# Moving the first batch's result stores to ScalarE's queue, and another order for the last projection

## The chip, the cores and the metric

The kernel runs on 1 core of one Trainium2 chip. The metric is the device time of one execution in microseconds (us). The engines are TensorE (PE for its matmuls, PEld for its weight loads), VectorE (DVE), ScalarE (ACT), GpSimd (POOL) and SyncE (SP, which here only issues DMAs). ACT and POOL can issue DMAs from their own queues too. Each engine works through its own list of instructions in order.

## The reference

Eight sequences of 3008 tokens and 256 channels pass through a spectral filter, and every token then passes through a gated feed-forward block:

```python
X = np.fft.rfft(x, axis=1)
Y = X * (filt_r + 1j * filt_i)[None]
y = np.fft.irfft(Y, n=3008, axis=1).reshape(8 * 3008, 256)
g = y @ w_gate                                   # 256 -> 1536
silu = g * (1.0 / (1.0 + np.exp(-g)))
out = (silu * (y @ w_val)) @ w_out               # 1536 -> 256
```

## The kernel before, in words

**Steps.** The feed-forward part of a batch is cut into 4 chunks of tokens (`k`) and the hidden width into 3 groups (`g`). One pair (k, g) is one step, so a batch has 12 steps and the kernel 96, and a last half step finishes what is left. In the first batch the first nine steps run over the chunks 0 to 2 for g = 0, then for g = 1, then for g = 2, and steps 9 to 11 are chunk 3; in the other batches the three groups of a chunk follow each other. In each step pieces of the next batch's Fourier work (`pa`, `pb`, `pc`, `pd`) are woven in. Steps are counted from 0 over the whole kernel.

**The order inside a step** is written out by hand: `SCHEDULE` (line 88) is a list of tokens, and each token emits a few instructions in this order to whichever engines do them. `P`, `Q`, `A`, `B`, `E` are products on PE (line 862); `f`, `c`, `m`, `g`, `u` are ACT's copies and activations out of PSUM; `D` (line 879) and `S` (line 913) are subtractions and additions on POOL; `s`, `x03`, `y`, `e`, `h`, `v`, `l` are mostly DVE. `W1` to `W7` are the seven products of the output projection (line 954) and `o1` to `o7` move or add a PSUM bank into the output tile (lines 966 and 968); `z0` to `z3` transpose its four parts in place on DVE (line 930), and `x0` to `x5` store the tile to DRAM, two DMAs each (line 943). A token with a prime belongs to the group two steps back (`older`) or to the previous group (`before`), as its place in the pipeline demands. So when a group's last hidden part is done in step s, its output is complete at the beginning of step s + 2 and is stored there, which happens for g = 2 alone.

**Queues of the stores.** Each of the 12 DMAs of a group stores up to 32 partitions in runs of 128 bytes. For the first batch they are issued from POOL, for the others from SP, and for the very last group they go around SP, ACT and POOL, in two halves (`x` and `X`). In the first batch groups with g = 2 are the steps 6, 7, 8 and 11, and their stores are issued in the steps 8, 9, 10 and 13, behind POOL's `S00'` and `S01'` and between its next subtractions.

**Preparation.** During the steps of the first batch the weights are rounded piece by piece. Line 1206 lets 20 ticks of that work happen in each step, at places spread evenly over the number of tokens in `SCHEDULE`.

**Banks of the projection.** `W1`, `W6`, `W7`, `W4` add up in one PSUM bank A, which `o1`, `o6`, `o7`, `o4` read in between; `W2` uses bank F, and `W5` and `W3` bank G. A product that adds into a bank waits until the reader before it is done. `S0` to `S3` make the four sums of the hidden tiles that `W5`, `W6`, `W7` and `W3` read. `LAST` (line 99) is the order of this for the final group; there all eight sums are on DVE (line 1246).

Of the kernel before, what the change touches and what calls it, by code (L numbers as in the profile page):

```python
# [64 lines left out]
NG = 3  # L65
# [20 lines left out]


SCHEDULE = """
Q0 o3' z1.o' t4.2' W2 f0 S00' S01' x0.o' t0.0 x1.o' Q1 t0.1 x2.o' P3 x3.o' f1 t4.3' W1 x4.o' S10' x03 S11'
s13 x5.o' P1 o1 t0.2 P0 o2 z0.o c1 D01 A13 g1 c0 S20' Q2 S21' g0 y01 m13 t1.0 h0 f2 s01 W6 t1.1 h1 x23  # L90
D02 P2 o6 D12 A01 c2 B13 g2 n3' m01 t0.3 S30' t1.2 x02 W7 S31' g13 y12 y02 B01 h13 o7 t1.3 t2.0 s02
s12 g01 h2 Q3 t2.1 h01 e12 A02 y23 W4 e02 y03 m02 g3 A12 o4 z2.o t2.2 E12 m12 B02 t2.3 l12 E02 u12 e13
g02 t3.0 h3 s23 l02 B12 v12 E13 t3.1 h02 u02 A23 n2 l13 g12 v02 W5 s03 e23 h12 e01 m23 A03 o5
z3.o u13 E23 t3.2 m03 v13 E01 l23 e03 t3.3 t4.0 l01 u23 B23 v23 u01 t4.1 E03 n1 v01 g23 B03 l03 W3 h23 g03
u03 h03 v03
""".split()
KS = (-1, 0, 1, 2)

LAST = """
S00 S01 S10 S11 W1 o1 W2 o2 z0.o S20 S21 S30 S31 W6 o6 W5 o5 W3 o3 z1.o x0.o x1.o x2.o x3.o x4.o  # L100
x5.o W7 o7 z3.o W4 o4 z2.o X0.o X1.o X2.o X3.o X4.o X5.o
""".split()
BLOCKS = (0, 1, 3, 2)
PAIRS = ((0, 1), (1, 2), (2, 3), (0, 2), (1, 3), (0, 3))
# [68 lines left out]
def kernel(  # L173
# [10 lines left out]
    nc = tc.nc  # L184
# [70 lines left out]
    def add(eng, dst, a, b):  # L255
        return eng.tensor_tensor(out=dst, in0=a, in1=b, op=ALU.add)  # L256
# [561 lines left out]
    def takes_turns(b, k):  # L818
        return b == 0 and k < NT

    def new_outs(b, k, g):
        outs[b, k] = opool.tile([128, 4 * NH, RP], FP32, name=f"o_{b}_{k}_{g}", tag="o", bufs=2)
        if g:
            pin(nc.sync.dma_start(out=outs[b, k], in_=o_dram[k]))
        else:
            pin(nc.gpsimd.memset(outs[b, k][:, :, NR:], 0.0))

    class Group:
# [94 lines left out]
        def project(self, op, last=False):  # L923

            b, k, q = self.b, self.k, self.g
            kind, p = op[0], int(op[1])
            if kind == "z":
                if q == NG - 1:
                    t = self.part(p)
                    pin(nc.vector.transpose(out=t, in_=t))  # L930
                return
            if kind in "xX":
                t, first, count = outs[b, k], 2 * NH * (kind == "X"), 2 * NH if last else 4 * NH
                if q < NG - 1 and takes_turns(b, k) and p == 5:
                    pin(nc.sync.dma_start(out=o_dram[k], in_=t))
                if q == NG - 1:
                    for n, (u, cq) in enumerate(divmod(m, 4) for m in (2 * p, 2 * p + 1)):
                        rows = min(32, NR - 32 * u)
                        at = (b * S + 32 * 32 * u + 2 * NH * k) * C + 128 * first + 32 * cq
                        queue = nc.sync if b else nc.gpsimd  # L940
                        if last:
                            queue = (nc.sync, nc.scalar, nc.gpsimd)[(2 * p + n) % 3]
                        pin(queue.dma_start(  # L943
                            out=bass.AP(tensor=out.tensor, offset=out.offset + at,
                                        ap=[[32 * C, rows], [128, count], [1, 32]]),
                            in_=t[32 * cq:32 * cq + rows, first:first + count, ts(u, 32)]))
                return
            at = {1: "A", 6: "A", 7: "A", 4: "A", 2: "F", 5: "G", 3: "G"}[p]
            if kind == "W":
                start = p in (1, 2, 5)  # L950
                if start:
                    self.bank(at, 3)
                for i in range(JB):
                    pin(nc.tensor.matmul(  # L954
                        out=self.tiles[at], lhsT=wo_t[:, JB * q + i, WO[p], :],
                        rhs=self.hs[i][:, HID[p]], start=start and i == 0,
                        stop=True, skip_group_check=True))
                return
            if q == 0 and p == 1:
                new_outs(b, k, q)  # L960
            i, cb = {1: (0, 0), 2: (0, 0), 6: (0, 1), 3: (0, 1), 4: (1, 0), 7: (1, 1),
                     5: (1, 1)}[p]
            dst = self.part(2 * i + cb)[:, :, 0:NR].rearrange("p n (t r) -> p t n r", t=2)
            src = self.tiles[at].rearrange("p (t n r) -> p t n r", t=2, n=NH)
            if q == 0 and at == "A":
                pin(nc.scalar.copy(out=dst, in_=src))
            else:
                pin(add(nc.vector, dst, dst, src))
# [7 lines left out]
    x0 = [t[0:NR, 8 * C * i:8 * C * i + 8 * C] for t, i in ((wo_f, 0), (wo_f, 1), (y_f, 0))]  # L976
    x0 = [t.rearrange("p (n c) -> p n c", c=C) for t in x0]
# [6 lines left out]
    with tc.tile_pool(name="start", bufs=1) as spool0:  # L984
# [3 lines left out]
        f0 = spool0.tile([128, NS, C], FP32, name="f0")  # L988
# [8 lines left out]
        n = 0  # L997
# [68 lines left out]
        for p in ("A13", "A01"):  # L1066
            at = SLOT[p]
# [29 lines left out]
    older = before = None  # L1097
    pieces_before = []

    def order_of(b):  # L1100

        steps = [divmod(step, NG) for step in range(NCHUNK * NG)]
        if b == 0:
            steps[:NT * NG] = [(k, g) for g in range(NG) for k in range(NT)]
        return steps
# [45 lines left out]
    for b in range(B):  # L1151
# [36 lines left out]
        for step in range(NCHUNK * NG + (b == B - 1)):  # L1188
            ghost = step == NCHUNK * NG
            k, g = order_of(b)[min(step, NCHUNK * NG - 1)]  # L1190
            this = None
            pieces = []
            if not ghost:
                pieces = plan[step]
                this = Group(b, k, g, cur.y[k], sequence_of(cur, nxt, step))
                if b == 0:
                    preparation.finish(step)
                chunk = {0: 1, 2: 2, 5: 3}.get(step)
                if b and chunk:
                    cur.load_t4(chunk, 0)  # L1200
            elif before is None:
                break
            ends = {ORDER[e - 1]: n for n, (_, e) in enumerate(PIECES)}
            last = ghost or b == B - 1 and step == NCHUNK * NG - 1
            for place, token in enumerate(SCHEDULE):
                if b == 0 and this and place * TICKS % len(SCHEDULE) < TICKS and \
                        (step or place > SCHEDULE.index("A01")):
                    preparation.tick(step)
                old = token.endswith("'")
                op = token.rstrip("'")  # L1210
                if op[0] == "t":
                    n = int(op[1])
                    ps = pieces_before if old else pieces
                    if n < len(ps):
                        next(ps[n], None)
                elif op[0] in "Wo" or op.endswith(".o"):

                    g0 = older if old else before
                    if g0 is not None and (old or not ghost):
                        g0.project(op)  # L1220
                else:
                    g0 = before if old else this
                    if g0 is not None and not (ghost and op[0] == "S"):
                        g0.step(op)
                if old or this is None:
                    continue
                if nxt and (step, op) == ((4, "P2") if b else (5, "A23")):
                    nxt.load_two(0)
                if b + 2 < B and (step, op) in ((10, "Q2"), (10, "B01"), (11, "Q2")):

                    following.load_x(2 if step == 11 else int(op == "B01"))
                if b + 2 < B and step == 11 and op in ("A02", "B02"):
                    following.pair(int(op == "B02"))
                if b and chunk and op == "B01":
                    cur.load_t4(chunk, 1)
                for i in range(2):
                    if nxt and (step, op) == (10, ("A12", "E23")[i] if b else "E23"):
                        nxt.load_t4(0, i)
                for f, args in chores.get((step, op), ()) if b == 0 else ():
                    f(*args)  # L1240
                if op in ends and not last and (b or step >= NT * NG - 1):
                    reload_weights((g + 1) % NG, ends[op])
            older, before, pieces_before = before, this, pieces
    for op in LAST:
        if op[0] == "S":
            older.step(op, nc.vector)
        else:
            older.project(op, True)
# [28 lines left out]
```

## Time and profile before

| | us |
|---|---|
| median of 7 runs (lowest to highest) | 2897.09 (2895.87 to 2899.42) |
| the profiled execution, its own time | 2896.33 |
| its span in the profile | 2894.6 |
| busy in the span: PE, DVE, ACT, POOL | 2843.9, 2075.3, 1577.8, 1532.0 |
| 48 stores of the first batch, POOL's time for one: least, median, most | 0.651, 0.664, 0.838 |
| 8 stores of the last group on ACT: least, median, most | 0.374, 0.466, 0.493 |

The profile lists for stretches of time how long each engine was busy, and in its timeline what each engine did in order, with the idle time before an instruction and what ended it in brackets. An instruction that only issues a DMA is shown as ACTq or SPq; POOL's DMA issues appear as POOL's own time. The share behind "DMA" is the mean busy share of the 16 DMA engines.

### The profile page before, as it was taken

The numbers are of one execution on the slowest core, as the hardware profiler recorded it, in microseconds if no ns is written. First come the engines' busy times: TensorE is split into PE (matmuls) and PEld (weight loads), VectorE is DVE, ScalarE is ACT, GpSimd is POOL, SyncE is SP. The second block draws the span as 40 slices with busy tenths as digits, with TensorE's granted clock in tenths as the row PEclk, the third lists the DMA queues.
The fourth block names the chain that finished last, engine by engine and source line by source line (L and its number), as shares of the span: only waits on it lengthen the run. The fifth ranks groups of instructions, "written<-read, shape, count | busy, mean of one in ns | idle before, by whom it ended". The sixth has DMA issues, their size and how long they took to land.

```text
span 2894.6 us, 47312 instructions
## 1 busy us (share of the span) xinstructions
PE 2843.9 (98%) x14784; PEld 2433.9 (84%) x14784; DVE 2075.3 (72%) x4664; ACT 1577.8 (55%) x4190; POOL 1532.0 (53%) x1669
## 2 busy tenths in 40 slices
PE   7999999999999999999999999999999999999998
PEld 5777778888888888888888888888888888888886
DVE  6888766777677767777767677677677767766666
ACT  6775445555555555555555554555555555555553
POOL 4886665454545454446453555544554544555443
PEclk9999999999999999999999999999999999999999
DMA  8687865666666665667556566566665666645443
GB/s 232 213 267 245 288 195 162 189 210 197 194 180 191 220 188 185 192 185 218 193 176 202 175 215 204 177 197 182 211 190 192 184 205 194 208 141 163 145 137 80
DMA packets 396367, 558.89 MB, mean 193 GB/s; under 512 B 201079, under 2 KB 296585, under 8 KB 396117
## 3 DMA queue, kind: packets, MB, share of 16 engines
q1 hardware_dynamic: 366533, 506.80, 56.8%
q10 hardware_dynamic: 27792, 45.72, 4.7%
q0 software_dynamic: 1792, 3.34, 0.4%
q8 instruction: 120, 1.97, 0.3%
q14 instruction: 130, 1.06, 0.1%
HBM read 460.38 MB, written 95.34 MB: 192 GB/s over the span
## 4 chain that ended last, share of the span: by engine, by line
PE 88%; POOL 4%; DVE 2%; issue 2%; ACT 0%; POOLq 0%; DVEq 0%
PE wa L862 24%; PE wA L954 16%; PE wk L862 15%; PE we L862 12%; PE wG L954 8%; PE wF L954 4%; PE pd L765 3%; PE pc L731 2%; PE pb L698 2%; POOL out_dram L943 1%; PE pa L639 1%; PE pa L641 1%; POOL h L259 1%; POOL h L256 0%; POOL y_t L256 0%
## 5 line engine op out<-in xcount | busy, mean ns | idle before, releaser
L862 PE MATMUL wa<-y_t,wt_t 128*128 128x188 f32 x4464 | 879.7, 323 | 9.4 <-DVE wa L884 6.2
L862 PEld LDWEIGHTS wa<-y_t,wt_t 128*128 128x128 f32 x4464 | 749.3, 190 | 91.3 <-ACT wa L888 10.0
L256 POOL TENSOR_TENSOR h<-h 128x376 f32<-128x376 f32 x190 | 184.7, 993 | 778.0 <-DVE h L909 778.0
L862 PEld LDWEIGHTS wk<-y,wt_t 128*128 128x128 f32 x2976 | 501.0, 190 | 80.0 <-DVE y L256 0.5
L862 PE MATMUL wk<-y,wt_t 128*128 128x188 f32 x2976 | 565.0, 323 | 0.0
L259 POOL TENSOR_TENSOR h<-h 128x376 f32<-128x376 f32 x570 | 561.5, 1008 | 0.1
L954 PE MATMUL wA<-h,wo_t 128*128 128x376 f32 x1536 | 551.0, 481 | 8.5 <-POOL h L259 5.2
L862 PE MATMUL we<-y_t,wt_t 128*128 128x188 f32 x2232 | 431.6, 323 | 0.8 <-ACT we L893 0.7
L259 DVE TENSOR_TENSOR we<-we,m 128x376 f32<-128x376 f32 x576 | 316.7, 555 | 135.5 <-PE we L862 86.1
L954 PEld LDWEIGHTS wA<-h,wo_t 128*128 128x128 f32 x1536 | 279.8, 190 | 115.5 <-POOL h L259 9.2
L862 PEld LDWEIGHTS we<-y_t,wt_t 128*128 128x128 f32 x2232 | 369.4, 190 | 1.4 <-ACT we L893 1.0
L259 POOL TENSOR_TENSOR D<-f,f 128x376 f32<-128x376 f32 x288 | 281.6, 989 | 132.4 <-ACT f L877 124.2
L897 ACT COPY m<-wa 128x376 f32<-128x376 f32 x576 | 272.0, 472 | 86.5 <-PE wa L862 83.7
L263 DVE SCALAR_TENSOR_TENSOR y<-wk,c 128x376 f32<-128x376 f32 x480 | 244.0, 540 | 85.5 <-ACT we L893 56.9
L904 ACT ACTIVATE u<-we 128x188 f32<-128x188 f32 x576 | 189.0, 328 | 191.1 <-DVE we L259 171.2
L954 PE MATMUL wG<-h,wo_t 128*128 128x376 f32 x768 | 274.0, 479 | 1.2 <-DVE o L256 1.2
L904 ACT ACTIVATE g<-wa 128x188 f32<-128x188 f32 x576 | 187.5, 327 | 160.3 <-PE wa L862 144.7
L877 ACT ACTIVATE f<-wk 128x376 f32<-128x376 f32 x288 | 139.5, 484 | 223.5 <-PE wk L862 155.5
L881 ACT COPY c<-wk 128x376 f32<-128x376 f32 x288 | 136.2, 473 | 221.7 <-PE wk L862 221.7
L884 DVE SCALAR_TENSOR_TENSOR x<-wk,f 128x376 f32<-128x376 f32 x192 | 104.3, 543 | 201.7 <-PE wk L862 199.6
L893 ACT COPY we<-y 128x376 f32<-128x376 f32 x480 | 221.3, 479 | 39.9 <-DVE h L909 24.8
L909 DVE TENSOR_TENSOR h<-wa,g 128x188 f32<-128x188 f32 x576 | 197.0, 346 | 31.6 <-ACT g L904 30.7
(157 smaller groups left out, 3854.2 us busy)
## 6 DMA issues: line engine op xcount, KB each, us to landing
wt_t<-w_all SPq DMA_DIRECT2D x174, 896.0 KB
wt_t<-w_all SPq DMA_DIRECT2D x174, 768.0 KB
lent<-later_tbl SPq DMA_DIRECT2D x84, 256.0 KB
lent<-in_filt_r_dram SPq DMA_DIRECT2D x336, 64.0 KB
d<-lent ACTq DMA_DIRECT2D x84, 256.0 KB
d<-t ACTq DMA_DIRECT2D x78, 240.0 KB
lent<-d SPq DMA_DIRECT2D x144, 128.0 KB
t<-d SPq DMA_DIRECT2D x112, 128.0 KB
```

The costliest lines, as they stand in the source:

```text
L256: return eng.tensor_tensor(out=dst, in0=a, in1=b, op=ALU.add)
L259: return eng.tensor_tensor(out=dst, in0=a, in1=b, op=ALU.subtract)
L263: return nc.vector.scalar_tensor_tensor(out=dst, in0=a, scalar=-1.0, in1=b, op0=ALU.mult, op1=ALU.subtract)
L862: pin(nc.tensor.matmul(out=ps[:, z], lhsT=self.wt[:, SLOT[p], z], rhs=rhs, start=start and z == 0, stop=True, skip_group_check=True))
L877: pin(act.mul(self.small(f"f{i}", f"f{i}", 1), t[f"k{i}"], -1.0))
L881: pin(act.copy(out=self.small(f"c{i}", f"c{i}", 1), in_=t[f"k{i}"]))
L884: pin(v.scalar_tensor_tensor(out=dst, in0=t[f"k{j}"], scalar=-1.0, in1=t[f"f{i}" if j == 3 else f"D{at}"], op0=ALU.mult, op1=ALU.add))
L893: pin(act.copy(out=self.bank(f"e{at}"), in_=t[f"y{at}"]))
L897: pin(act.copy(out=self.small(f"m{at}", "m", 4), in_=t[f"a{at}"]))
L904: pin(act.activation(out=self.small(op, "g", 3, 1)[:, 0], in_=ps[:, 1], func=AF.Silu))
L909: pin(v.tensor_tensor(out=dst, in0=ps[:, 0], in1=g, op=ALU.mult))
L954: pin(nc.tensor.matmul(out=self.tiles[at], lhsT=wo_t[:, JB * q + i, WO[p], :], rhs=self.hs[i][:, HID[p]], start=start and i == 0, stop=Tru ...
```

## The change

Twelve tokens `i0` to `i11` are added to `SCHEDULE`. In a step whose `older` group belongs to the first batch and has g = 2, each of them issues one of the twelve stores from ACT's queue; the tokens `x0.o'` to `x5.o'` no longer store anything there. They stand between the other tokens from place 8 to place 66 of the now 166 (154 before). The ticks of the preparation stay 20 per step, and as they are spread over the number of tokens they move by up to 7 tokens ahead. In the final group the order of sums and products is another, the two sums `S20` and `S21` go to POOL, `W4` starts a bank of its own (F), and `o4`'s work is split: `q4` adds what bank A holds, and `o4` later adds bank F.

```diff
 SCHEDULE = """
-Q0 o3' z1.o' t4.2' W2 f0 S00' S01' x0.o' t0.0 x1.o' Q1 t0.1 x2.o' P3 x3.o' f1 t4.3' W1 x4.o' S10' x03 S11'
-s13 x5.o' P1 o1 t0.2 P0 o2 z0.o c1 D01 A13 g1 c0 S20' Q2 S21' g0 y01 m13 t1.0 h0 f2 s01 W6 t1.1 h1 x23
-D02 P2 o6 D12 A01 c2 B13 g2 n3' m01 t0.3 S30' t1.2 x02 W7 S31' g13 y12 y02 B01 h13 o7 t1.3 t2.0 s02
...
+Q0 o3' z1.o' t4.2' W2 f0 S00' S01' i0 x0.o' t0.0 x1.o' i1 Q1 t0.1 x2.o' P3 i2 x3.o' f1 t4.3' W1 i3
+x4.o' S10' x03 S11' i4 s13 x5.o' P1 i5 o1 t0.2 P0 o2 i6 z0.o c1 i7 D01 A13 g1 c0 i8 S20' Q2 S21' g0
+y01 m13 t1.0 h0 i9 f2 s01 W6 t1.1 h1 i10 x23 D02 P2 o6 D12 A01 i11 c2 B13 g2 n3' m01 t0.3 S30' t1.2
...
 LAST = """
-S00 S01 S10 S11 W1 o1 W2 o2 z0.o S20 S21 S30 S31 W6 o6 W5 o5 W3 o3 z1.o x0.o x1.o x2.o x3.o x4.o
-x5.o W7 o7 z3.o W4 o4 z2.o X0.o X1.o X2.o X3.o X4.o X5.o
+S00 S01 W1 S20 S21 S10 S11 W5 o1 W2 o5 S30 S31 W6 o2 z0.o o6 W3 o3 z1.o x0.o x1.o x2.o x3.o x4.o
+x5.o W7 q4 o7 z3.o W4 o4 z2.o X0.o X1.o X2.o X3.o X4.o X5.o
...
-                if q == NG - 1:
-                    for n, (u, cq) in enumerate(divmod(m, 4) for m in (2 * p, 2 * p + 1)):
+                if q == NG - 1 and (b or kind == "i"):
+                    some = (p,) if kind == "i" else (2 * p, 2 * p + 1)
+                    for n, (u, cq) in enumerate(divmod(m, 4) for m in some):
...
-                        queue = nc.sync if b else nc.gpsimd
+                        queue = nc.sync if b else nc.scalar
...
-            at = {1: "A", 6: "A", 7: "A", 4: "A", 2: "F", 5: "G", 3: "G"}[p]
+            if kind == "q":
+                at, kind, p = "A", "o", 4
+            else:
+                at = {1: "A", 6: "A", 7: "A", 4: "F" if last else "A", 2: "F", 5: "G",
+                      3: "G"}[p]
             if kind == "W":
-                start = p in (1, 2, 5)
+                start = p in (1, 2, 5) or last and p == 4
...
+                if op[0] == "i":
+                    if older is not None and older.b == 0:
+                        older.project(op)
...
-            older.step(op, nc.vector)
+            older.step(op, nc.gpsimd if op[1] == "2" else nc.vector)
```

More of the change, by code (lines that the diff above doesn't have):

```diff
@@ L88 @@
 SCHEDULE = """
-Q0 o3' z1.o' t4.2' W2 f0 S00' S01' x0.o' t0.0 x1.o' Q1 t0.1 x2.o' P3 x3.o' f1 t4.3' W1 x4.o' S10' x03 S11'
-s13 x5.o' P1 o1 t0.2 P0 o2 z0.o c1 D01 A13 g1 c0 S20' Q2 S21' g0 y01 m13 t1.0 h0 f2 s01 W6 t1.1 h1 x23
-D02 P2 o6 D12 A01 c2 B13 g2 n3' m01 t0.3 S30' t1.2 x02 W7 S31' g13 y12 y02 B01 h13 o7 t1.3 t2.0 s02
[L92 to L95, printed above, removed]
+Q0 o3' z1.o' t4.2' W2 f0 S00' S01' i0 x0.o' t0.0 x1.o' i1 Q1 t0.1 x2.o' P3 i2 x3.o' f1 t4.3' W1 i3
+x4.o' S10' x03 S11' i4 s13 x5.o' P1 i5 o1 t0.2 P0 o2 i6 z0.o c1 i7 D01 A13 g1 c0 i8 S20' Q2 S21' g0
+y01 m13 t1.0 h0 i9 f2 s01 W6 t1.1 h1 i10 x23 D02 P2 o6 D12 A01 i11 c2 B13 g2 n3' m01 t0.3 S30' t1.2
+x02 W7 S31' g13 y12 y02 B01 h13 o7 t1.3 t2.0 s02 s12 g01 h2 Q3 t2.1 h01 e12 A02 y23 W4 e02 y03 m02
+g3 A12 o4 z2.o t2.2 E12 m12 B02 t2.3 l12 E02 u12 e13 g02 t3.0 h3 s23 l02 B12 v12 E13 t3.1 h02 u02
+A23 n2 l13 g12 v02 W5 s03 e23 h12 e01 m23 A03 o5 z3.o u13 E23 t3.2 m03 v13 E01 l23 e03 t3.3 t4.0 l01
+u23 B23 v23 u01 t4.1 E03 n1 v01 g23 B03 l03 W3 h23 g03 u03 h03 v03
 """.split()
@@ L925, in project @@
             b, k, q = self.b, self.k, self.g
-            kind, p = op[0], int(op[1])
+            kind, p = op[0], int(op[1:].split(".")[0])
             if kind == "z":
@@ L931, in project @@
                 return
-            if kind in "xX":
+            if kind in "xXi":
                 t, first, count = outs[b, k], 2 * NH * (kind == "X"), 2 * NH if last else 4 * NH
-                if q < NG - 1 and takes_turns(b, k) and p == 5:
+                if kind == "x" and q < NG - 1 and takes_turns(b, k) and p == 5:
                     pin(nc.sync.dma_start(out=o_dram[k], in_=t))
-                if q == NG - 1:
-                    for n, (u, cq) in enumerate(divmod(m, 4) for m in (2 * p, 2 * p + 1)):
+                if q == NG - 1 and (b or kind == "i"):
+                    some = (p,) if kind == "i" else (2 * p, 2 * p + 1)
+                    for n, (u, cq) in enumerate(divmod(m, 4) for m in some):
                         rows = min(32, NR - 32 * u)
                         at = (b * S + 32 * 32 * u + 2 * NH * k) * C + 128 * first + 32 * cq
-                        queue = nc.sync if b else nc.gpsimd
+                        queue = nc.sync if b else nc.scalar
                         if last:
@@ L1210 @@
                 op = token.rstrip("'")
-                if op[0] == "t":
+                if op[0] == "i":
+                    if older is not None and older.b == 0:
+                        older.project(op)
+                elif op[0] == "t":
                     n = int(op[1])
```

## The prediction

> **What bounds the kernel now.** I read the page first: busy times, then the chain that ended last.
>
> ```profile
> PE 2843.9 (98%) x14784; PEld 2433.9 (84%) x14784; DVE 2075.3 (72%) x4664; ACT 1577.8 (55%) x4190; POOL 1532.0 (53%) x1669
> ...
> PE 88%; POOL 4%; DVE 2%; issue 2%; ACT 0%; POOLq 0%; DVEq 0%
> ```
>
> PE is busy 98% of the span and is 88% of the chain. An edit off PE can only win where PE stands still, so the question is where that is. The chain by line names one oddity: POOL's store `out_dram` (line 943) with 1% of the span, though stores produce nothing that is computed with. I therefore cut the time into steps, from the first `W2` product of a step to that of the next, and asked for each engine's busy time in each. Columns: the stretch and its length; then busy us and, in brackets, the number of instructions of PE, PEld, DVE, ACT, POOL; last the granted clock, the DMA share and GB/s.
>
> ```profile
> 293.10:322.80 29.70, 29.70 (x154) 25.66 (x153) 24.14 (x53) 14.28 (x38) 12.85 (x14) 1.00 0.89 306
> 322.80:360.10 37.30, 32.91 (x154) 26.34 (x153) 24.46 (x53) 15.70 (x41) 27.83 (x32) 0.95 0.87 279
> 360.10:394.70 34.60, 30.74 (x154) 25.45 (x154) 24.52 (x54) 14.98 (x40) 23.78 (x30) 1.00 0.70 217
> 394.70:427.60 32.90, 29.91 (x151) 24.67 (x150) 18.52 (x43) 16.56 (x43) 21.02 (x27) 1.00 0.61 189
> 427.60:456.20 28.60, 28.60 (x158) 25.03 (x158) 19.83 (x49) 15.01 (x41) 17.06 (x18) 1.00 0.41 131
> 456.20:485.80 29.60, 29.60 (x158) 25.67 (x158) 22.69 (x52) 15.96 (x43) 13.00 (x15) 1.00 0.60 192
> 485.80:518.10 32.30, 30.35 (x157) 25.58 (x157) 17.80 (x45) 17.19 (x44) 18.38 (x25) 1.00 0.56 171
> ...
> 604.50:633.30 28.80, 28.80 (x149) 24.81 (x149) 21.94 (x49) 15.04 (x40) 20.02 (x20) 1.00 0.66 207
> ```
>
> These are the steps 7 to 13, and step 17. Equal matmul counts take equal time except in steps 8, 9, 10 and 13, the four in which POOL issues twelve stores each. **The excess**: step 8, 37.3 - 29.7 (154 matmuls, as in step 7) = 7.6; step 9, 34.6 - 29.7 = 4.9; step 10, 32.9 - 28.8 (as step 17) = 4.1; step 13, 32.3 - 29.6 (as step 12) = 2.7. Sum **19.3 us**. The timelines of POOL and of PE in step 8 say how:
>
> ```profile
> 322.01 1.93 POOL L256 TENSOR_TENSOR h<-h 128x376 f32<-128x376 f32 x2 [8.86 <-DVE h L909]
> 323.88 5.36 POOL L943 DMA_DIRECT2D out_dram<-o  x8
> ...
> 335.16 0.99 POOL L259 TENSOR_TENSOR D<-f,f 128x376 f32<-128x376 f32 x1
> ```
>
> ```profile
> 336.80 1.54 PE L862 MATMUL wa<-y_t,wt_t 128*128 128x188 f32 x8 [1.39 <-DVE wa L884]
> 339.48 2.72 PE L954 MATMUL wA<-h,wo_t 128*128 128x376 f32 x4 [1.14 <-DVE o L256]
> ```
>
> POOL spends 12 x 0.685 = 8.2 us (its mean in this step) issuing stores ahead of `D01`, which DVE needs for `s01`, which PE needs for `A01`. Between 340 and 350 us the granted clock is also 0.85, so about 1.5 us of the 7.6 are matmuls at a lower clock after three pauses; these go with the pauses. The Trainium skill, "TensorE: Matmul & The Clock Gate", Part 1, puts the fall to half rate at an idle window of about 3.4 us; no pause here is longer than 1.54 us, so what the row shows is finer than the rule.
>
> **Part 1, stores off POOL: -19.3 us.** All 48 issues leave POOL. What is then late next? POOL's other work in step 8 is 27.8 - 8.2 = 19.6 us, and step 17 runs without a pause at 20.0 us on POOL. The 8.86 us that POOL idled before step 8 return as reserve. So POOL should drop out, and PE be last again.
>
> **Part 2, the same stores on ACT: +4 us, between 1.2 and 23.** On ACT one issue takes 0.374 to 0.493 us (8 in the last group), 12 x 0.466 = 5.6 us per step; with that ACT is at 21.3 of 29.7 us. The stores wait for `z1.o'`, a DVE transpose that in step 8 starts at 322.91 and lasts 0.58, so it ends at 323.49, where ACT's `f0` (323.02, 0.48) ends too; `z0`, `z2`, `z3` are a step older. So the data hold nobody. The place on ACT, from a step without stores (step 18, ACT's timeline):
>
> ```profile
> 633.59 0.48 ACT L877 ACTIVATE f<-wk 128x376 f32<-128x376 f32 x1 [1.42 <-PE wk L862]
> 636.35 0.48 ACT L877 ACTIVATE f<-wk 128x376 f32<-128x376 f32 x1 [2.28 <-PE wk L862]
> 638.83 0.47 ACT L881 COPY c<-wk 128x376 f32<-128x376 f32 x1 [1.99 <-PE wk L862]
> ```
>
> `i0` to `i2` (1.4 us) fit into the 2.28 us that ACT waits ahead of `f1`, `i3` to `i6` (1.9 us) into the 1.99 us ahead of `c1`. `i7` and `i8` stand in a run without gaps (up to 0.47 us each, less if the issue overlaps the running copy), `i9` ahead of a gap of 0.17, `i10` and `i11` (0.9 us) ahead of one of 1.31. That is at most about 1 us of delay per step, for `g1`, `c0`, `g0`, `m13` and whoever waits for them.
>
> The second cost is a wait that the change adds. The trace's records show SP's and ACT's DMAs using the same eight completion semaphores in turn, POOL's eight others; a DMA waits until the one eight before it has landed. The stores now take turns with SP's bursts of eight loads. Behind a waiting store on ACT stand `f1`, `c1`, `g1`, and PE, DVE and POOL behind those. From below: of ACT's 182 DMAs with a compute producer, 6 start later than their producer's end by over 0.2 us, 4.6 us in all, longest 1.13; at that mean 48 stores cost 1.2 us. From above: a store landed 2.4 to 5.8 us after its issue; one whole such wait per step is 4 x 5.8 = 23 us. A gain is excluded, as ACT only receives work. I take 4, one us per step, close to the lower row because that is ACT on these same semaphores, and above it because the stores add 12 turns to the 37 that SP and ACT have in step 8. SP in its turn can run ahead of ACT by fewer loads.
>
> DMA capacity belongs to this: step 8 used 0.87 x 37.3 = 32.5 us of all 16 engines, more than the 29.7 us it would have left. Loads issued early can move into step 9 (0.70 x 34.6 = 24.2 of 29.7), so I count nothing beyond the 4 but give it to a rival.
>
> The Trainium skill, "DMA: Bandwidth & Descriptors", Issuing engines are not separate DMA queues, speaks against the change: all issuers share the 16 engines, and another issuer saves issue time only, usually little. By that rule part 1 would be worth an estimated 48 x (0.685 - 0.466) = 10 us; the rows decide for more, since POOL's issues stand ahead of what PE waits for and ACT's mostly in idle time.
>
> **Part 3, ticks of the preparation: 0, between -2 and +3.** 20 ticks per step as before, up to 7 tokens earlier. Steps 1 to 6 hold pauses of PE of 8.6 us in all; the moved ticks can change a fifth of that downwards or a third upwards. I see no reason for a sign.
>
> **Part 4, the last projection: -2.7 us.** The end before:
>
> ```profile
> 2885.64 1.53 PE L954 MATMUL wA<-h,wo_t 128*128 128x376 f32 x4 [0.64 <-DVE o L256]
> 2887.21 0.55 DVE L256 TENSOR_TENSOR o<-o,wA 128x376 f32<-128x376 f32 x1 [1.01 <-PE wA L954]
> ```
>
> `W4` waits for `o7`, and `o4` for `W4`; `z2` starts at 2887.79. The new order, with a DVE sum at 0.46, a PSUM addition at 0.47 to 0.58 and a product pair at 1.27 on PE and 1.46 until DVE may read: `S00` to `S11` to 2877.6, `o1`, `o5`, `S30`, `S31`, `o2`, `z0` to 2880.6, `o6` to 2881.1; `W3` readable at 2881.7, then `o3`, `z1` to 2882.8; `W7` readable at 2882.9, `q4`, `o7`, `z3` to 2884.5, while `W4` runs beside them and is readable at 2884.2; so `o4` at 2884.5 and `z2` at 2885.07, which is 2887.79 - 2885.07 = 2.7 earlier. `q4` is one DVE addition more (0.47), in this sum. `S20` and `S21` on POOL (0.99 each) end near 2878.4 and are needed at 2881.2: hidden, and 2.8 us would have to go wrong first. The stores behind `z2` are the same. Bounds: 1.5 to 3.
>
> **Sum** against the profiled execution: 2896.33 - 19.3 + 4 + 0 - 2.7 = 2878.3. The median of the runs is 0.76 above that execution: **2879.1**.
>
> **Rivals.** (a) The forecast, 0.68: 2874 to 2884. (b) Loads come late, 0.20: with shared semaphores and no pause to hide in, step 8 lasts its 32.5 us of DMA (+2.8), step 9 loses likewise, and ACT waits; for it speaks DVE's wait of 1.6 us for a load at 362.4, against it that steps 10 and 13 have shares of 0.61 and 0.56. About 8 us more: 2887. (c) It doesn't do what it says, 0.06: PE's pauses come from the loads of the first batch, not from POOL, and only the end improves: 2897.1 - 2.7 = 2894.4. Against it: step 7 has the highest DMA share of all, 0.89, and no pause. (d) Slower, 0.06: ACT, in order, is held by a store whose semaphore belongs to a load that SP itself can't yet issue. It decides from (19.3 + 2.7) / 4 = 5.5 us per step beyond ACT's slack; two waits of 5.8 us in each of four steps are 46 us: 2897 - 22 + 46 = 2921.
>
> **Numbers.** A measurement of this kernel tells 0.2% (5.8 us) from no change. Faster: (a) and (b), 0.88; same: (c), 0.06; slower: (d), 0.06. Range: down to no cost on ACT and 2 us from the ticks, 2897.1 - 22 - 2 = 2873; up to half the upper bound of part 2 and 3 from the ticks, 2897.1 - 22 + 11.6 + 3, about 2889; outside are (c), (d) and the edges of (a) and (b).
>
> **What would show it.** Right: the four steps at 29.7, 29.7, 28.8 and 29.6 us within 1, no POOL store before the last group, ACT's stores at 0.37 to 0.5 us, `z2` 2.7 us closer to the last product of the main loop. Wrong: ACT idle ahead of a store until a DMA lands, DVE's line 707 waiting for loads in steps 8 and 9, or steps 1 to 6 of other lengths.

## The result and the profile after

The kernel after takes **2904.69 us** (median of 13 runs, 2900.19 to 2908.12), the kernel before in the same runs 2896.32 (median of 33 runs, 2894.09 to 2899.67). The ratio is **1.0028, 95% interval 1.0021 to 1.0035**: slower by 0.28%, where the forecast was 2879. The profiled execution took 2904.41 us, its span is 2902.6, which is 8.0 more than before.

The page, in the lines that answer to those of before, and the two queues that changed (before, q10 had 27792 packets and 4.7%, q0 1792 and 0.4%):

```profile
PE 2848.6 (98%) x14784; PEld 2440.3 (84%) x14784; DVE 2079.1 (72%) x4663; ACT 1577.7 (54%) x4190; POOL 1503.4 (52%) x1623
...
q10 hardware_dynamic: 52608, 48.80, 5.4%
...
q0 software_dynamic: 256, 0.25, 0.0%
```

POOL is 28.6 us less busy: 48 DMA issues are gone, and two sums have come. PE is busy for 4.7 us more with the same 14784 matmuls; the granted clock of the steps 8, 9 and 10 below is 0.91, 0.87 and 0.95, before it was 0.95, 1.00 and 1.00. And q0 has lost 1536 packets with the stores, while q10 has gained 24816.

The same steps 7 to 10 and 13 as in the prediction, columns as there (11 and 12 last 28.6 and 29.6 us as before):

```profile
296.00:325.70 29.70, 29.70 (x154) 25.66 (x153) 24.13 (x53) 14.28 (x38) 12.86 (x14) 1.00 0.87 305
325.70:364.40 38.70, 33.71 (x154) 27.67 (x153) 24.28 (x53) 15.61 (x41) 19.88 (x20) 0.91 0.86 264
364.40:403.90 39.50, 32.66 (x153) 27.88 (x153) 24.87 (x54) 14.63 (x40) 15.88 (x18) 0.87 0.65 190
403.90:438.50 34.60, 30.86 (x150) 26.25 (x149) 18.82 (x43) 16.45 (x43) 13.25 (x15) 0.95 0.59 173
...
496.70:528.20 31.50, 30.17 (x158) 25.49 (x157) 18.87 (x45) 16.86 (x44) 10.99 (x13) 1.00 0.64 176
```

The same four steps, 8, 9, 10 and 13, are the long ones. From product to product (the stretches above are rounded to a tenth) step 8 went from 37.3 to 38.7 us, step 9 from 34.6 to 39.6, step 10 from 32.9 to 34.6, step 13 from 32.4 to 31.5. The 8.0 us of the span are then: +2.6 ahead of step 1, +0.3 in steps 1 to 7, **+7.2 in steps 8 to 13**, -0.3 in steps 14 to 94, -1.8 behind them. POOL's pause has gone and something else stands in its place.

What stands there is shown by three timelines of step 9. First ACT (start, length, what it did; in brackets the idle time ahead of it and what ended it):

```profile
367.40 0.48 ACT L877 ACTIVATE f<-wk 128x376 f32<-128x376 f32 x1 [2.28 <-DVE lent L707]
368.13 3.46 ACTq L944 DMA_DIRECT2D out_dram<-o  x4
371.63 0.47 ACT L881 COPY c<-wk 128x376 f32<-128x376 f32 x1 [3.75 <-DMA out_dram<-o]
...
379.79 0.34 ACTq L944 DMA_DIRECT2D out_dram<-o  x1
380.17 0.48 ACT L877 ACTIVATE f<-wk 128x376 f32<-128x376 f32 x1 [6.03 <-DMA lent<-in_filt_r_dram]
```

Then SP, and PE:

```profile
371.78 0.34 SPq L407 DMA_DIRECT2D wt_t<-w_all  x1
...
373.07 6.10 SPq L530 DMA_DIRECT2D lent<-in_filt_r_dram  x4
```

```profile
372.45 1.43 PE L959 MATMUL wA<-h,wo_t 128*128 128x376 f32 x4
380.71 1.62 PE L862 MATMUL wk<-y,wt_t 128*128 128x188 f32 x4 [6.84 <-ACT f L877]
```

The store at 379.79 is `i9`. It has nothing to do with the load `lent<-in_filt_r_dram` that the bracket names. But the records show that it uses the completion semaphore which that load used last (SP and ACT take eight of them in turn), and it starts 0.02 us after the load landed. The load was issued at 373.07 behind 896 KB of weights issued at 371.78, which landed at 378.83. `i9` stands right ahead of `f2` on ACT, PE's next product adds into the bank that `f2` reads, and PE works in order: so a store waiting for its turn stopped PE for 6.84 us. In the stretch from 300 to 530 us ACT's idle time ended with a landing of no concern to its own work in three kinds of places (columns: us in total, times, longest):

```profile
ACT c L881 <- DMA out_dram<-o: 12.9, 3, 5.9
...
ACT f L877 <- DMA lent<-in_filt_r_dram: 6.0, 1, 6.0
...
ACT f L877 <- DMA wt_t<-w_all: 3.7, 1, 3.7
```

Together 22.6 us. (The line `c<-wk` is charged because it is the first piece of work behind the waiting store; the view doesn't count the store itself as work. So these gaps hold the issuing of the stores too; and the name isn't always that of the DMA waited for: the longest, 5.9 us, ends behind a store whose last wait was for the load `lent<-later_tbl`.) The semaphores' own records say whose turn it was: the stores waited some 23 us in the four steps, about 17 of it for loads of SP's and 6 for ACT's own earlier stores.

The pause has a second price, the clock, in the windows of step 9 behind it:

```profile
380.70:383.00 2.30, 2.29 (x7) 2.29 (x8) 0.99 (x2) 0.72 (x2) 2.27 (x3) 0.50 0.80 208
383.00:386.00 3.00, 3.00 (x9) 2.42 (x9) 1.82 (x4) 1.98 (x7) 2.40 (x4) 0.50 0.43 99
386.00:389.00 3.00, 3.00 (x16) 2.58 (x15) 1.83 (x4) 1.14 (x3) 2.03 (x3) 0.95 0.00 0
```

After 6.84 us without work PE runs at a granted clock of 0.50 for some 5.6 us (the first two windows and a tenth of the third), and its busy time in the step is 3.0 us more than 29.7. Of the 9.9 us that step 9 is too long, 6.84 are the pause and 3.0 the clock. The Trainium skill, "TensorE: Matmul & The Clock Gate", Part 1, has the clock at half after an idle window of about 3.4 us: this row agrees. In step 8 of `no_first_stores` below, whose only pause is 2.07 us long, the granted clock falls too, to 0.95 over the step, which that rule doesn't tell.

### The profile page after: what moved, and what is told of

The parts are those of the page before. It is cut to its first block, busy times and chain, and to the rows that moved or that the text cites. A ratio compares the mean times of both kernels' runs of the same rounds, so it can differ in the third digit from the quotient of the medians.

```text
span 2902.6 us, 47289 instructions
## 1 busy us (share of the span) xinstructions
PE 2848.6 (98%) x14784; PEld 2440.3 (84%) x14784; DVE 2079.1 (72%) x4663; ACT 1577.7 (54%) x4190; POOL 1503.4 (52%) x1623
## 4 chain that ended last, share of the span: by engine, by line
PE 89%; DVE 1%; DMA 1%; POOL 1%; issue 0%; ACT 0%; ACTq 0%; SPq 0%; POOLq 0%; DVEq 0%
PE wa L862 24%; PE wA L959 16%; PE wk L862 16%; PE we L862 12%; PE wG L959 8%; PE wF L959 4%; PE pd L765 3%; PE pc L731 3%; PE pb L698 2%; PE pa L639 1%; PE pa L641 1%; DVE o L256 0%; DMA lent<-in_filt_r_dram 0%; DVE o L930 0%; DVE lent L714 0%
## 5 line engine op out<-in xcount | busy, mean ns | idle before, releaser
L862 PE MATMUL wk<-y,wt_t 128*128 128x188 f32 x2976 | 567.7, 324 | 15.2 <-ACT f L877 15.2
L259 POOL TENSOR_TENSOR h<-h 128x376 f32<-128x376 f32 x572 | 565.1, 1011 | 15.2 <-DVE h L256 15.2
L893 ACT COPY we<-y 128x376 f32<-128x376 f32 x480 | 220.9, 479 | 36.4 <-DVE h L909 23.8
L909 DVE TENSOR_TENSOR h<-wa,g 128x188 f32<-128x188 f32 x576 | 197.0, 346 | 32.2 <-ACT g L904 31.3
```

Source lines behind the costliest of these rows:

```text
L259: return eng.tensor_tensor(out=dst, in0=a, in1=b, op=ALU.subtract)
L862: pin(nc.tensor.matmul(out=ps[:, z], lhsT=self.wt[:, SLOT[p], z], rhs=rhs, start=start and z == 0, stop=True, skip_group_check=True))
L893: pin(act.copy(out=self.bank(f"e{at}"), in_=t[f"y{at}"]))
L909: pin(v.tensor_tensor(out=dst, in0=ps[:, 0], in1=g, op=ALU.mult))
```

## The experiments

The expectations use three short names. T0: the new end of the kernel made it slower. T1: ACT's stores wait for their turn at a completion semaphore, behind loads that are late; in its first form, late because of the weights that are loaded again in these steps. T2: it is the stores' own weight, their small pieces, that ACT or its queue pays for. Step lengths are in us from the profiles; each ratio is to the kernel before, measured beside it, with its 95% interval.

### One part of the change at a time

`stores_only` has the stores on ACT and before's end; `last_only` has only the new end; `ticks_only` has the tokens in `SCHEDULE`, where they do nothing, so that only the preparation's ticks move.

```diff
 # ticks_only, against before; SCHEDULE as after
-                if op[0] == "t":
+                if op[0] == "i":
+                    pass
+                elif op[0] == "t":
```

> The change without its last projection: the twelve stores of each first-batch group on ACT, one by one, old end. Theory T1 (ACT's stores wait for a turn of the eight completion semaphores that they share with SP's loads, and the loads land late): steps 8, 9, 10, 13 as in the changed kernel (38.7, 39.6, 34.6, 31.5 us), total 1.8 us above the changed kernel, about +10 us on the kernel before. Rival T0 (the new end makes it slower): no slower than the kernel before.

> The other half alone: old stores on POOL, new last projection. By the sum of the prediction -2.7 us; by the changed profile, whose last step begins 9.8 us late and whose end is 8.0 us late, -1.8 us. Rival T0: slower than before.

> The kernel before with the twelve tokens in SCHEDULE doing nothing, so only the ticks of the preparation move; stores as before. By the profiles so far (steps 1 to 7 last 220.4 to 220.7 us in the kernels with moved ticks, 219.6 in most without) +1 us; if the moved ticks also make the time ahead of step 1 longer (102.9 to 107.8 against 102.4 to 104.8) +2 to +3.

Measured: `stores_only` 2906.59, ratio 1.0039 (1.0026 to 1.0051); `last_only` 2894.15, 0.9995 (0.9986 to 1.0004); `ticks_only` 2898.53, 1.0010 (1.0001 to 1.0019). T0 falls: the new end alone costs nothing that can be seen, and the stores alone show the whole loss (steps 8, 9, 10 and 13 take 41.5, 37.3, 35.9 and 31.3 us, 1.7 more in all than in the kernel after and split otherwise). The moved ticks cost 2.9 us (0.3 to 5.5). Only a small part of it is in steps 1 to 7, which take 220.8 us against 220.4; the rest lies ahead of step 1, where the profiled executions of kernels with moved ticks differ by 4.9 us among themselves and the others by 2.4, so that it isn't shown to come from the ticks.

### What the stores cost on either engine

`no_first_stores` is the kernel before without the 48 stores; `stores_sp` is the kernel before with SP as their issuer, at their old places.

```diff
-                if q == NG - 1:
+                if q == NG - 1 and b:                      # no_first_stores
...
-                        queue = nc.sync if b else nc.gpsimd
+                        queue = nc.sync                    # stores_sp
```

> The kernel before without the 48 stores of the first batch (its results are left out of the output). If POOL's issues are the whole cause of the pauses in steps 8, 9, 10 and 13: those steps last 29.7, 29.7, 28.8, 29.6 us and the total falls by 19.3. If the loads bound step 8 (32.5 us of DMA work): step 8 stays near 32.5 and the total falls by some 12 to 16.

> The kernel before with the first batch's stores issued from SP, as in the other batches, at their old places in the order. T1 and its rival T2 (what holds ACT is the issuing itself: issue time and full rings) both say that a wait on SP holds only SP: POOL and ACT free, -15 to -19 us, unless SP's loads then come late (DVE line 707 waiting for loads), which would give back up to 10.

`no_first_stores`: 2879.9, ratio 0.9947 (0.9934 to 0.9959). Its steps 8, 9, 10 and 13:

```profile
323.10:357.60 34.50, 32.15 (x154) 26.53 (x154) 24.58 (x53) 15.59 (x41) 19.91 (x20) 0.95 0.77 262
357.60:387.30 29.70, 29.70 (x154) 25.66 (x153) 24.70 (x54) 14.62 (x40) 15.98 (x18) 1.00 0.77 244
387.30:416.50 29.20, 29.06 (x149) 24.80 (x149) 18.52 (x43) 16.34 (x43) 13.17 (x15) 1.00 0.54 179
...
474.70:504.30 29.60, 29.60 (x158) 25.68 (x157) 18.54 (x45) 17.10 (x44) 10.99 (x13) 1.00 0.51 160
```

These are the steps without stores: 14.1 us shorter in all than before (steps 8 to 13), not the 19.3 that the prediction took as the excess. The difference is step 8, which keeps 4.8 us, because PE waits there for a load that has nothing to do with the stores:

```profile
335.67 1.66 PE L862 MATMUL wa<-y_t,wt_t 128*128 128x188 f32 x8 [2.07 <-DMA y_t<-yt]
```

Measured against these steps, the stores on ACT cost 4.2, 9.9, 5.3 and 1.9 us, **21.3 in all**, where the stores on POOL cost 14.1. That is the +7.2.

`stores_sp`: 2906.07, 1.0038 (1.0025 to 1.0050). A waiting store now holds nobody but SP, and the time is as bad. Its steps 8 and 11:

```profile
324.30:367.80 43.50, 32.52 (x154) 27.07 (x153) 24.52 (x53) 15.59 (x41) 19.77 (x20) 0.88 0.76 236
431.60:469.50 37.90, 30.85 (x157) 26.95 (x157) 19.79 (x49) 15.01 (x41) 17.19 (x18) 0.91 0.53 168
```

Behind the stores on SP stand the loads: in step 8 PE waits 9.4 us for `lent<-d`, in step 11 PE's `pd` product waits for `t<-d`. My expectation here, that late loads give back at most 10 of the 15 to 19 us, was wrong: SP's order of issue is what the loads depend on, though SP computes nothing.

### Turns, bytes or packets

`stores_tiny` and `stores_quarter` are the kernel after with 1 or 4 of the 16 runs of 128 bytes of each row stored: the same 48 DMAs, in the same places and turns. `no_reload` leaves out the repeated loads of the weights in the first batch. `stores_runs` stores all bytes, but into a scratch area of DRAM, in rows of 2048 bytes in one piece.

```diff
+                    count = 1 if kind == "i" else count            # tiny; quarter: 4
...
-                if op in ends and not last and (b or step >= NT * NG - 1):
+                if op in ends and not last and b:                  # no_reload
...
+                            pin(queue.dma_start(                   # runs
+                                out=scratch[12 * k + p, 0:rows],
+                                in_=flat[32 * cq:32 * cq + rows, ts(u, 512)]))
```

> The changed kernel with each of the 48 stores cut to a sixteenth of its bytes (one run of 128 bytes per row in place of sixteen; the rest of the first batch's result is left out). As many DMAs, in the same turns of the shared semaphores. T1 (ACT waits for its turn behind loads that land late): ACT still starts stores some 20 ns after the DMA before them on their semaphore has landed, steps 8 to 10 stay within 4 us of 38.7, 39.6, 34.6, total +4 to +8 us on the kernel before. T2 (the issuing of large stores holds ACT): steps 8, 9, 10 and 13 fall to about 34.5, 29.7, 29.2, 29.6 as without stores, total about -15 us.

> The changed kernel with each store cut to a quarter (four runs of 128 bytes per row; the rest is left out). T3 and T1b both say between the sixteenth (-13 us) and the whole (+8): about -8 to -12 us if the landing time grows with the number of packets.

> The changed kernel without the reloads of the weights in the first batch's steps 8 to 11 (the products there use weights that stand in the buffer, so the results are others). T1: with the 896 KB loads gone, loads and stores land within about 3 us, ACT's waits of 3 to 6 us go, steps 8, 9, 10 at 32 to 34, 30 to 31, 29 to 30 us, total -12 to -18 us. T2: stores are issued as before, steps stay near 38.7, 39.6, 34.6, total about +8.

> The changed kernel with each first-batch store of the same bytes taken as one run of 2048 bytes per row, into a scratch tensor in DRAM (so the first batch's result is left out), in place of sixteen runs of 128. Same issuer, places, number of DMAs and turns. T3 (the small packets, which take turns packet by packet with the loads' large ones, make the stores land late, and the turns behind them wait): ACT's waits nearly vanish as with the sixteenth, steps 8, 9, 10, 13 near 34.7, 29.9, 29.2, 30.1, total -11 to -14 us on the kernel before. T1b (the bytes, in whatever packets): steps as in the changed kernel, +5 or more.

Ratios: `stores_tiny` 2882.79, 0.9955 (0.9942 to 0.9969); `stores_quarter` 2884.80, 0.9963 (0.9949 to 0.9977); `no_reload` 2896.23, 1.0003 (0.9994 to 1.0012); `stores_runs` 2887.01, 0.9968 (0.9955 to 0.9981). The quarter lies between the sixteenth and the whole, nearer the sixteenth, as expected. In steps 8, 9, 10 and 13, worked out from ACT's and the DMAs' records:

| | ACT waits for a landing | ACT's issuing of 12 stores | longer than without stores |
|---|---|---|---|
| after | 7.2, 9.4, 4.8, 1.3 | 8.7, 5.1, 4.9, 8.2 | 4.2, 9.9, 5.3, 1.9 |
| `stores_tiny` | 0.5, 1.4, 0.4, 1.7 | 5.0, 5.7, 4.6, 4.5 | 0.2, 0.2, 0, 0.5 |
| `stores_runs` | 0.8, 2.7, 4.4, 2.1 | 5.0, 5.1, 4.8, 4.7 | 0, 0.2, 1.4, 0.8 |

Three readings. **Issuing twelve stores costs little by itself**: `stores_tiny` spends 4.5 to 5.7 us of ACT per step on it, as the prediction had it, and loses 0.9 us in the four steps together. **Waiting is the loss in steps 9 and 10**, 15.2 of the 21.3 us: PE's one long pause in each, 6.84 and 3.58 us, stands behind a store that waits for a load (step 9 above; in step 10 for `wt_t<-w_all`, 3.7 us). In steps 8 and 13 the first column doesn't tell it: in step 13 it is larger in the two runs that lose less. There it is ACT's issuing that takes over 3 us longer, mostly in three issues of 1.4 to 2.9 us against a median of 0.45. Two of them stand ahead of step 8's `f2`, and PE's longest pause of that step is the wait for it:

```profile
334.62 2.87 ACTq L944 DMA_DIRECT2D out_dram<-o  x1
...
337.81 1.36 ACTq L944 DMA_DIRECT2D out_dram<-o  x1
339.21 0.48 ACT L877 ACTIVATE f<-wk 128x376 f32<-128x376 f32 x1 [1.00 <-issue]
```

```profile
339.75 1.62 PE L862 MATMUL wk<-y,wt_t 128*128 128x188 f32 x4 [3.65 <-ACT f L877]
```

In step 13 PE's pause for `f2` is 1.18 us, and the long issue comes behind `f2`; how much of the loss there comes from the wait of 1.3 us and how much from the issuing isn't separated. And **both shrink with the number of packets**: `stores_runs` moves the same bytes with as many DMAs from the same places, and its step 9 takes 29.9 us, 0.2 more than without stores (the stretch here ends a little before the step does):

```profile
359.40:389.10 29.70, 29.70 (x153) 25.42 (x152) 24.37 (x54) 14.41 (x40) 15.79 (x18) 1.00 0.82 277
```

Its stores go to another place in DRAM, in one piece; that this has a part of its own isn't excluded, but `stores_tiny`, which writes to the old one, says the same. A step's base is not exact either: step 8 takes 32.8 us in `stores_quarter`, 1.7 less than without stores.

The records price the packets. From ACT the 3.08 MB go out in 24816 packets, nearly all of 128 bytes, and take 19.6 us of all 16 DMA engines; from POOL they go out in 752 data packets of 4 KB and take 11.3. A store lands 5.0, 4.3, 3.1 and 4.2 us after its issue in the four steps, in `stores_tiny` after 3.0, 3.6, 2.4 and 3.6, in `stores_runs` after 2.9, 3.8, 3.7 and 3.9.

The first form of T1 is too small: without the weights' reloads the time falls by some 7 us of the 21 that `stores_tiny` gives back (by the ratios). Steps 9 and 10 fall to 34.8 and 29.2 us, but step 8 takes 41.0, and ACT still waits 9.8 us in it, over half of it behind SP's load `y<-y`. T2 as ACT's own time holds in part, in steps 8 and 13. What holds is a mixture: ACT waits for turns, as T1 says, and they are long on account of the small pieces, as T2 says.

### Issuer and place, apart

`pool_late` issues the stores from POOL, one at a time, but late in the step, behind `S31'`; the ticks stay where they were, and `new_outs` of step 8 moves from `Q3` to `A23` so that the tile is not taken too early. `act_late` is the same with ACT; both have the old end. `pool_spaced` is the kernel after with POOL as issuer, at the places of the change.

```diff
-D02 P2 o6 D12 A01 c2 B13 g2 n3' m01 t0.3 S30' t1.2 x02 W7 S31' g13 y12 y02 B01 h13 o7 t1.3 t2.0 s02
...
+h1 x23 D02 P2 o6 D12 A01 c2 B13 g2 n3' m01 t0.3 S30' t1.2 x02 W7 S31' i0 g13 i1 y12 y02 i2
+B01 h13 i3 o7 t1.3 i4 t2.0 s02 i5 s12 g01 i6 h2 Q3 i7 t2.1 h01 i8 e12 A02 i9 y23 W4 i10
...
-        chore(step, "Q3", lambda s: new_outs(0, *order_of(0)[s]), step)
+        chore(step, "Q3" if step < 2 * NT + 2 else "A23", lambda s: new_outs(0, *order_of(0)[s]), step)
```

> The kernel before with the stores still on POOL, one by one, but behind S31' and so in the second half of the step, where POOL idles (the reload of step 8's output tile moves behind them, ticks of the preparation stay at their places). T1 and T2: POOL's DMAs have eight semaphores of their own, nothing waits on ACT; steps near 34.5 to 36, 29.7 to 31, 29.2 and 29.6, total -10 to -15 us. If instead what costs is the DMA traffic of the stores itself, whoever issues them: no better than -5.

> The kernel with the stores behind S31' in the second half of the step (2882.7 us from POOL), issued from ACT: only the issuer differs. T1: ACT waits for turns again, stores start some 20 ns after the landing of the DMA before them, at least one step over 33 us in place of 29.7, total 5 to 15 us above the version on POOL. If only the place ahead of f2 was bad: within 2 us of it.

> The changed kernel with the twelve stores issued from POOL at the very places where it issues them from ACT: same bytes, same times, another issuer with semaphores of its own. T1 (ACT's turns behind SP's loads): no wait on ACT, POOL's 8 us of issuing are spread, steps 8 to 10 between those without stores (34.5, 29.7, 29.2) and before (37.3, 34.6, 32.9), total -3 to -10 us. If the stores' traffic makes the loads late whoever issues them: steps 8 to 10 as in the changed kernel, +5 or more.

| | steps 8, 9, 10, 13 | time | ratio |
|---|---|---|---|
| POOL, place of the change | 36.7, 36.3, 30.9, 30.7 | 2892.35 | 0.9990 (0.9981 to 0.9999) |
| ACT, place of the change (after) | 38.7, 39.6, 34.6, 31.5 | 2904.69 | 1.0028 (1.0021 to 1.0035) |
| POOL, late | 36.4, 29.7, 29.2, 29.6 | 2882.74 | 0.9955 (0.9941 to 0.9969) |
| ACT, late | 44.6, 33.3, 30.8, 36.9 | 2905.49 | 1.0035 (1.0023 to 1.0047) |

At either place ACT is the worse issuer of these stores, by 12 us (11 by the ratios) and by 23. `pool_spaced` is above what was expected of it in step 9. Step 8 of `pool_late`, then of `act_late`:

```profile
322.10:358.50 36.40, 32.32 (x154) 27.07 (x153) 24.62 (x53) 15.60 (x41) 27.85 (x32) 0.95 0.86 286
```

```profile
323.80:368.40 44.60, 34.79 (x155) 28.23 (x154) 24.65 (x53) 15.74 (x41) 19.90 (x20) 0.89 0.76 231
```

POOL is busy for 27.85 us in step 8 with all twelve issues, as before the change, and three of the four steps still have no loss: the 8 us of issuing were never the trouble, only their place ahead of `D01` and what hangs on it. That they stood in one piece was a small part: spread out at the change's places (`pool_spaced`) they still cost 11.5 us in the four steps, of 14.1. POOL's eight completion semaphores are its own, so a late load of SP's holds none of its stores. What these runs can't do is vary the issuer without its semaphores and its packets, or the other way round; and the packets matter. With runs of 2048 bytes, stored to the scratch area, ACT loses 2.4 us in the four steps at the change's places (`stores_runs`), less than POOL's 11.5 there, so ACT is not the worse issuer of every store.

### The end of the kernel

`last_dve` is `last_only` with all eight sums on DVE. `best` puts this end on `pool_late`.

```diff
-            older.step(op, nc.gpsimd if op[1] == "2" else nc.vector)
+            older.step(op, nc.vector)
```

> The new last projection alone, with all eight sums on DVE. In the changed kernel DVE's sums S10 and S11 took 2.57 us beside POOL's S20 and S21, 0.54 each before. If POOL slows them: they take 1.0 us again, S20 and S21 add 0.9, and the last transpose starts about 10.8 us after the first addition of the end, in place of 11.5 in the changed kernel and 12.5 before; total -1.6 us. If they are slow by their place in the order: still about 2.5 us, and the end no earlier than 12.

> Stores on POOL in the second half of the step and the new last projection with all sums on DVE: -13.1 and -1.7 us add up, since they lie 2400 us apart: about -15 us on the kernel before.

`last_dve`: 2893.62, 0.9994 (0.9985 to 1.0002). `best`: **2881.91, 0.9954 (0.9942 to 0.9967)**, faster than before and after both, by 13.8 us where about 15 were expected; the end's own share in it can't be told from `pool_late`. The traces tell more than the times. From DVE's last product of the hidden tiles to the start of the last transpose it takes 12.76 us before, 11.78 after and in `last_only`, and 11.07 in `last_dve` and `best`. The reason stands in the end's timeline, after and in `last_dve`:

```profile
2886.34 2.40 POOL L259 TENSOR_TENSOR h<-h 128x376 f32<-128x376 f32 x2 [15.17 <-DVE h L256]
2886.57 2.57 DVE L259 TENSOR_TENSOR h<-h 128x376 f32<-128x376 f32 x2
```

```profile
2876.76 1.93 DVE L259 TENSOR_TENSOR h<-h 128x376 f32<-128x376 f32 x4
```

Beside POOL's two sums, DVE's two take 2.57 us; without them DVE does four in 1.93. Giving two sums to POOL saves DVE nothing.

## Why the prediction was wrong

- **Part 1 (-19.3)**: the mechanism was right, the size was 14.1. The step lengths of before were compared with step 7, which does not wait for its loads; step 8 does (2.07 us for `y_t`, and a lower clock after it), and 4.8 of its 7.6 us stay without any store. The other 0.4 is step 10.
- **Part 2 (+4, measured +21.3): the step that failed.** It named the right wait, the eight completion semaphores taken in turn, and priced it wrongly, in four ways. It took the price from ACT's DMAs of the kernel before (0.025 us each), and these are mostly packets of 2 KB, whereas the stores bring 24816 small ones. It kept 23 as the upper bound, which is close to what came, and then chose the end next to it by "the row on the same semaphores", though the row differs in what the DMAs carry and stand among. It priced `i9`'s place as a delay of at most 1 us by ACT's own gaps, without asking who waits for `f2`: PE does, in order, with nothing else to do. And it took 5.6 us per step for the issuing, which measured 8.7 and 8.2 in steps 8 and 13; two long issues, not a wait, stand ahead of PE's 3.65 us in step 8.
- **What takes over**, rival (d), given 0.06: ACT in order, held by a store whose turn belongs to a load. It came about with the sign of (d) and not with its size: 21.3 us in four steps, 5.3 per step, where (d) said that it decides from 5.5 per step with both gains whole (22 us). With the gains as measured, 14.1 and about 1, it decides from 3.8. In one detail (d) is not what happened: in step 9 the load had been issued by SP and was on its way; the wait was for its landing. The waits behind ACT's own earlier stores (some 6 of 23 us) and the long issues were not in (d) at all.
- **Part 3 (0)**: measured +2.9 (0.3 to 5.5), at the upper bound taken, and not traced to a step.
- **Part 4 (-2.7)**: 1.0 in the trace. The mis-sized term is "`S20` and `S21` on POOL: hidden". They were hidden as waits, but `S10` and `S11` beside them took 1.3 us each instead of the 0.46 of the sum; with the sums on DVE, which adds two of 0.46 to the prediction's chain, it is 1.7.
- **Together** the parts missed by 5.2, 17.3, 2.9 and 1.7 us, 27.1 in all; the change was forecast at -18.0 us and measured at +8.4, 26.4 apart.
- The forecast's tests worked: "ACT idle ahead of a store until a DMA lands" was listed as the sign of its failure, and it is what the trace shows.
- In the prediction a page was weighed that says that another issuer saves issue time only, usually little. The runs are on its side about ACT: nothing was won by its shorter issue. A sentence of the same page would have helped more. The Trainium skill, "DMA: Bandwidth & Descriptors", Anatomy of one DMA — SWDGE (gpsimd) path, says that DMA engines don't wait on semaphores: "any semaphore wait happens on the issuing sequencer before dispatch". ACT's row at 380.17, 6.03 us idle for a load of SP's, agrees.

**What stays open.** How small packets make the turns so long is not settled. Part of it may be that the stores land later (5.0 against 2.9 us in step 8), part that the turns are then handed out in another order: in `stores_tiny` and `stores_runs` other DMAs stand ahead of the same stores, and in steps 8 and 9 of both no store waits for a load of SP's. The turns also hold SP: in step 8 of the kernel after its loads wait 6.7 us for stores of ACT's, before for none. One of them, `lent<-later_tbl`, was issued 3.0 us late at 340.88 behind a store, and the store at 345.20 then waited 3.25 us for that load. The Trainium skill, "DMA: Bandwidth & Descriptors", Queues, rings and completion order, has each DMA engine take one packet from each queue in turn; a queue of 128-byte packets beside one of large loads would then get few bytes per turn, which fits the landing times of step 8 but was not measured here by itself; nor does a run show whether the 128-byte records of the trace are packets in the page's sense, which may hold several descriptors. Why three of ACT's issues in the kernel after took 1.4 to 2.9 us is unexplained. A store in fewer, larger DMAs was not tried.

## What to carry to other kernels

A DMA issued from a compute engine can hold that engine until an unrelated DMA has landed: before moving one, ask whose completion semaphore it takes, who stands behind it in the engine's order, and whether PE waits for that; a slack of a few tenths of a microsecond does not cover a landing of several. Where an engine's issues stand in front of something needed, moving them later on the same engine can be worth more (13.1 us here) than moving them to an engine with more idle time (8.4 lost with the whole change, 10.9 in `stores_only`). And to price a cost, take the kernel without the operation as the base, not a neighbouring step that differs in its loads.

## What the runs showed of the hardware

- The same store went out as 128-byte packets from ACT's queue (12.6 ns each, 19.6 us of the 16 engines in all) and as 4 KB packets from POOL's (241 ns each, 11.3 us): the issuer changed the cost of the transfer, not only who pays for its issue.
- DVE's sum of two tiles in SBUF (128x376, 4 bytes) took 1.32 and 1.33 us beside POOL's sums, 0.54 alone. From 2886.34 to 2889.14, 2.80 us, both engines did two each; one after the other, at 0.99 and 0.46, these are 2.90. The Trainium skill, "SBUF — State Buffer", SBUF: two separate sides, has a port pair that DVE with two SBUF inputs and POOL lock for a whole instruction; the row fits that.
